# Attention feeding a bilinear layer on one core: the first conversions' Abs kept in order, three loads on another queue, PV and reciprocals moved ahead of the feed-forward slices

## The chip, the cores and the metric

One core of one Trainium2 chip. The metric is the device time of one execution in microseconds (us); lower is better. Before the change the median of three runs is 761.27 us (760.38 to 761.89).

## What is computed

Softcapped attention, then a bilinear feed-forward layer, all in fp32 (weights arrive as 64-bit floats):

```python
scores = cap * tanh((q @ k.T / sqrt(64)) / cap)      # 4 batches, 12 heads, 448 tokens, 64 wide
attn = exp(scores - max) / (sum + 1e-9)
x = (attn @ v) as 1792 tokens x 768
out = ((x @ w_a) * (x @ w_b)) @ w_out                # d_ff 1536
```

## The kernel before, in words

The 48 heads are worked as 24 **pairs** (two heads share the 128 partitions). Pairs 0 to 11 are group 0, pairs 12 to 23 group 1; a group gives 896 tokens of x. The kernel has three stretches: pairs 0 to 11 alone; pairs 12 to 23 beside the feed-forward of group 0; the feed-forward of group 1 alone.

The loop over `pi` (L478) runs a string of steps, one letter each: **P** `prep_pair(pi+1)` (transposes q and k on VectorE, L213; from pair 12 on splits them into a high and a low part), **S** and **T** `scores` for the first and second half of the keys (two PSUM tiles each: matmuls L239 or L244/L247, tanh on ScalarE L248, one exp L249, then sums of the probabilities on VectorE L253, or L256 and L257), **A** `attend(pi-1)` (PV matmuls L269, L271), **N** `normalize(pi-1)` (row sums by matmul L282, reciprocal L290, stored to DRAM L291 and read back spread over all partitions as `den` L295), **M** `scale` (L301, PV times `den`; pinned in program order on VectorE), **F** a slice of the feed-forward (`run_ffn`, matmuls L403 to L405 and L434 to L436). From pair 13 on the string is `SFANFMTPF`: three feed-forward slices a pair.

Score tiles and, in the second stretch, the PV tile (`both`, L261) come from one PSUM pool of two buffers (`ps_sc`): while PV is held, from A to M, the scores have one buffer.

Weights: `load64` (L327) fetches a 768 KB chunk of 64-bit weights into one of two buffers; `ready_w` (L347) turns it into fp32: ScalarE Copy L361 and Abs L362, three VectorE operations L363 to L365, a GpSimd add L366, a store to DRAM L367; `split_w` (L372) makes high and low parts (L385, L386). In program order the first two chunks are loaded at the end of pi = 2 and the first four converted at the ends of pi = 8 to 11, three of them split at the end of pi = 11.

The order on each engine is not the program's: a planner lays it out at build time from its own estimates of durations, taking at each moment the ready instruction that is earliest in the program. `keep_in_program_order` pins one instruction behind the instruction traced before it on its engine. Pinned before the change: L361, L301 and the first two weight loads (on SP's queue). The Abs L362 is not pinned, and needs only its chunk's load and a free buffer. On the chip each engine keeps the planned order: an instruction that waits holds all behind it.

Of the kernel before, what the change touches and what calls it, by code (L numbers as in the profile page):

```python
# [14 lines left out]
AF = mybir.ActivationFunctionType  # L15
# [102 lines left out]
def kernel(  # L118
# [11 lines left out]
    nc = tc.nc  # L130
# [3 lines left out]
    P = 128  # L134
# [11 lines left out]
    NPG = NPAIR // NG  # L146
# [5 lines left out]
    AHEAD = 4  # L152
# [10 lines left out]
    capt = top.tile([P, 8], F32, tag="capt", name="capt")  # L163
# [13 lines left out]
    def f32(ap):  # L177
        return ap.bitcast(F32)
# [14 lines left out]
    def load_pair(pi):  # L193
        b, hp = divmod(pi, NP)
        for nm, src in (("k", k), ("q", q)):
            t = ld.tile([P, S // BLK, BLK], F32, tag=f"ld{nm}", name=f"ld{nm}_{pi}")
            for j in range(2):
                for h in range(D // BLK):
                    rows = slice(j * D + h * BLK, j * D + (h + 1) * BLK)
                    cols = src[b, 2 * hp + j, :, h * BLK : (h + 1) * BLK]  # L200
                    eng = nc.scalar if nm == "q" and pi == 0 else nc.sync
                    eng.dma_start(t[rows], cols.rearrange("(c p) d -> p c d", p=BLK))
            raw[nm, pi] = t
        t = ld.tile([P, 2 * NC3 + 1, D], F32, tag="ldv", name=f"ldv_{pi}", bufs=3)
        nc.sync.dma_start(t, v[b, 2 * hp : 2 * hp + 2].rearrange("j s d -> (j s) d").rearrange("(c p) d -> p c d", p=P))
        raw["v", pi] = t

    def prep_pair(pi):
        stk[pi] = []
        for nm in "kq":  # L210
            t = raw.pop((nm, pi))
            tt = qk.tile([P, S], F32, tag=f"t{nm}", name=f"t{nm}_{pi}")
            nc.vector.transpose(tt, t.rearrange("p c d -> p (c d)"))  # L213
            if pi >= NPG:
                hi = qk.tile([P, S], F32R, tag=f"h{nm}", name=f"h{nm}_{pi}", bufs=1)
                lo = qk.tile([P, S], F32R, tag=f"t{nm}", name=f"l{nm}_{pi}")
                nc.scalar.copy(hi, tt)
                nc.vector.tensor_sub(lo, tt, f32(hi))
                tt = (hi, lo)
            stk[pi].append(tt)  # L220
        if pi >= NPG:
            for z, x in zip(kz, stk[pi][0]):
                for j, o in enumerate(own):
                    nc.gpsimd.tensor_copy(z[o, j * R : (j + 1) * R], x[o, krem[j] : krem[j] + R])
# [73 lines left out]
    def scale(pi):  # L298
        g, r = divmod(pi, NPG)
        t, den = pvs.pop(pi)  # L300
        tc.keep_in_program_order(nc.vector.tensor_mul(den, t[:, :S], den))  # L301
        if g == 0:
            split_x(r, den, nc.gpsimd)
        else:
            nc.sync.dma_start(xd[r], den)
# [21 lines left out]
    def load64(eng):  # L327
        t = pos["raw"]
        if t >= NW:
            return  # L330
        pos["raw"] += 1
        nm, f, _ = seq[t]
        cs = slice(f * P, (f + 1) * P)
        w = {"a": w_a, "b": w_b, "o": w_out}[nm].bitcast(I32)
        rt = wp.tile([P, DM, 2], I32, tag="w64", name=f"w64{nm}_{f}", bufs=2)
        if nm == "o":
            ld64 = eng.dma_start(rt.rearrange("p n t -> p (n t)"), w[cs, :])
        else:
            ld64 = eng.dma_start(
                rt.rearrange("p (k f) t -> p k (f t)", k=NK),  # L340
                w.rearrange("(k p) f -> p k f", p=P)[:, :, 2 * f * P : 2 * (f + 1) * P],
            )
        if t < 2:
            tc.keep_in_program_order(ld64)
        wraw[t] = rt

    def ready_w():  # L347
        t = pos["conv"]
        if t >= len(seq):
            return  # L350
        pos["conv"] += 1
        nm, f, g = seq[t]
        if g:
            wt = wp.tile([P, DM], F32, tag="wt", name=f"wr{nm}_{f}", bufs=AHEAD)
            nc.sync.dma_start(wt, wd[nm, f])
            wfull[t] = wt
            return
        rt = wraw.pop(t)
        hw, lw = rt[:, :, 1], rt[:, :, 0]
        wt = wp.tile([P, DM], I32, tag="wt", name=f"wt{nm}_{f}", bufs=AHEAD)  # L360
        tc.keep_in_program_order(nc.scalar.activation(lw, lw.bitcast(U32), AF.Copy, scale=2.0**-29))  # L361
        nc.scalar.activation(f32(wt), f32(hw), AF.Abs)  # L362
        nc.vector.tensor_scalar_max(f32(wt), f32(wt), TINY_HI)  # L363
        nc.vector.tensor_scalar(wt, wt, 3, 0x3FFFFFFF, op0=ALU.logical_shift_left, op1=ALU.bitwise_and)
        nc.vector.scalar_tensor_tensor(wt, hw, -0x40000000, wt, op0=ALU.bitwise_and, op1=ALU.bitwise_or)  # L365
        nc.gpsimd.tensor_tensor(wt, wt, lw, op=ALU.add)  # L366
        nc.gpsimd.dma_start(wd[nm, f], f32(wt))  # L367
        wfull[t] = f32(wt)
        while pos["raw"] < min(t + 3, NW):
            load64(nc.gpsimd)  # L370
# [75 lines left out]

    with ExitStack():
        load_pair(0)
        nc.sync.dma_start(capt[:, 3:4], cap.rearrange("(a b) -> a b", b=1).to_broadcast([P, 1]))
        make_identity(nc, ident)  # L450
        load_pair(1)
        nc.vector.memset(sel, 0.0)
        for z in kz:
            nc.vector.memset(f32(z), 0.0)
        for m in range(2):
            nc.vector.memset(sel[:, m, m * Q // 2 : (m + 1) * Q // 2], 1.0)
        nc.vector.tensor_scalar_mul(capt[:, 4:5], capt[:, 3:4], -1.0)
        nc.vector.tensor_max(capt[:, 5:6], capt[:, 3:4], capt[:, 4:5])
        nc.vector.tensor_scalar(bounded, capt[:, 5:6], CAP_MAX, None, op0=ALU.is_le)
        nc.vector.tensor_scalar_min(capt[:, 0:1], capt[:, 5:6], CAP_MAX)  # L460
        nc.vector.reciprocal(capt[:, 6:7], capt[:, 0:1])
        nc.vector.tensor_scalar_mul(capt[:, 1:2], capt[:, 6:7], 1.0 / math.sqrt(D))
        nc.scalar.activation(capt[:, 7:8], capt[:, 0:1], AF.Exp, scale=-1.0)
        nc.vector.tensor_scalar_mul(capt[:, 2:3], capt[:, 7:8], 1e-9 / R)

        gen, done, p0 = None, 0.0, 0
        total = NF * 72 * S + NTI * 2 * NF * 3 * HALF

        def run_ffn(upto):
            nonlocal gen, done  # L470
            while gen is not None and done < upto:
                try:
                    done += next(gen)
                except StopIteration:
                    gen = None

        prep_pair(0)
        for pi in range(NPAIR + 1):  # L478
            order = "PASMNFTF" if pi < NPG - 1 else "ASMNFTPF" if pi <= NPG else "SFANFMTPF"
            slices = 0  # L480
            for step in order:
                if step == "P" and pi + 1 < NPAIR:
                    prep_pair(pi + 1)
                elif step == "A" and pi > 0:
                    attend(pi - 1)
                elif step == "N" and pi > 0:
                    normalize(pi - 1)
                elif step == "M" and (pi > NPG or pi > 1):
                    scale(pi - (1 if pi > NPG else 2))
                elif step == "S" and pi < NPAIR:  # L490
                    scores(pi, 0)
                    if pi + 2 < NPG - 1:
                        load_pair(pi + 2)
                elif step == "T" and pi < NPAIR:
                    scores(pi, 1)
                elif step == "F":
                    slices += 1
                    run_ffn(total * (pi - p0 + slices / order.count("F")) / (NPG + STRETCH))
            if pi == 2:
                load64(nc.sync)  # L500
                load64(nc.sync)
            if NPG - AHEAD <= pi < NPG:
                ready_w()
            if pi == NPG - 1:
                for _ in range(3):
                    split_w()
            if NPG - 1 <= pi + 2 < NPAIR:
                load_pair(pi + 2)
            if pi == NPG:
                scale(pi - 1)  # L510
            if pi and pi % NPG == 0:
                run_ffn(1e18)
                gen, done, p0 = ffn(pi // NPG - 1), 0.0, pi + 1
        run_ffn(1e18)
# [37 lines left out]
```

## Time and profile before

| | us |
|---|---|
| median of three runs | 761.27 |
| the profiled execution | 764.42 |
| its span, first to last instruction | 762.6 |
| PE (TensorE matmul) busy in the span | 717.4 |
| DVE (VectorE) busy | 454.7 |
| ACT (ScalarE) busy | 338.1 |
| POOL (GpSimd) busy | 256.0 |

Times in rows are microseconds from the span's start unless marked ns. PE is the matmul side of TensorE, SPq and POOLq are the instructions that issue DMAs. In a timeline row stand start, duration, engine, line, operation, written tile <- read tiles, count, and in brackets the idle time of the engine just before, with what ended it. The first feed-forward matmul (L403) runs at 127.0, the scaling of the last pair at 463.8. A busy share is an average over stretches with different limits, so a wait is read in the stretch in which it lies.

### The profile page before, as it was taken

How to read it: one execution, taken by the hardware profiler on the slowest of the kernel's cores; microseconds unless marked ns; L12 is line 12 of the kernel's file. 1: busy time of each engine (PE TensorE's matmuls, PEld its weight loads, DVE VectorE, ACT ScalarE, POOL GpSimd, SP SyncE). 2: the span in 40 equal slices, each digit the busy share in tenths (PEclk: the TensorE clock that was granted, in tenths of full speed). 3: DMA queues.
4: the chain of work that ended last, by engine and by line, in shares of the span. 5: the costliest groups of instructions: out<-in, count | busy, mean ns of one | idle time of the engine just before them, and what ended most of it. 6: DMA issues, size and time to landing. Idle time of an engine off the chain costs nothing.

```text
span 762.6 us, 10299 instructions
## 1 busy us (share of the span) xinstructions
PE 717.4 (94%) x3948; PEld 568.8 (75%) x3948; DVE 454.7 (60%) x588; ACT 338.1 (44%) x426; POOL 256.0 (34%) x220
## 2 busy tenths in 40 slices
PE   6979878998999999999979999999999999999996
PEld 2322224677677787778768789899999999999996
DVE  4788899987855798686777755732113333243222
ACT  5777888565765665375445541022322102202200
POOL 0011467486624775075561441012101201200100
PEclk9999989999999999999999999999999999999999
DMA  7585678666664577252452333632112102201012
GB/s 129 110 171 117 143 171 207 161 172 211 170 176 127 162 206 218 57 159 98 149 199 87 104 114 121 219 97 80 43 41 83 63 14 69 83 21 42 1 42 107
DMA packets 136951, 90.49 MB, mean 119 GB/s; under 512 B 114624, under 2 KB 122560, under 8 KB 136896
## 3 DMA queue, kind: packets, MB, share of 16 engines
q1 hardware_dynamic: 125856, 48.64, 25.7%
q0 software_dynamic: 9184, 40.90, 16.1%
q8 instruction: 33, 0.54, 0.3%
q10 hardware_dynamic: 1856, 0.23, 0.2%
q14 instruction: 22, 0.18, 0.1%
HBM read 67.24 MB, written 22.50 MB: 118 GB/s over the span
## 4 chain that ended last, share of the span: by engine, by line
PE 62%; DMA 15%; DVE 10%; issue 4%; SPq 3%; ACT 3%; POOL 3%; DVEq 0%; POOLq 0%; ACTq 0%
PE pha L404 7%; PE pha L403 6%; PE pha L405 6%; PE phb L405 6%; PE phb L403 6%; PE phb L404 6%; PE po L436 5%; PE po L434 5%; PE po L435 5%; PE pv L269 3%; DMA w64a<-in_moe_w_a_dram 3%; DMA rd<-rec 2%; DMA xl<-xd 2%; DMA ldq<-in_q_dram 2%; PE psc L244 2%
## 5 line engine op out<-in xcount | busy, mean ns | idle before, releaser
L434 PE MATMUL po<-who,gh 128*128 128x384 f32 x336 | 114.6, 341 | 5.3 <-DVE acc L440 3.3
L436 PE MATMUL po<-who,gl 128*128 128x384 f32 x336 | 113.2, 337 | 0.1
L435 PE MATMUL po<-wlo,gh 128*128 128x384 f32 x336 | 112.9, 336 | 0.0
L404 PE MATMUL pha<-xlo,wha 128*128 128x448 f32 x288 | 105.2, 365 | 0.0
L403 PE MATMUL pha<-xhi,wha 128*128 128x448 f32 x288 | 105.0, 364 | 0.0
L405 PE MATMUL phb<-xhi,wlb 128*128 128x448 f32 x288 | 104.9, 364 | 0.0
L403 PE MATMUL phb<-xhi,whb 128*128 128x448 f32 x288 | 104.8, 364 | 0.0
L404 PE MATMUL phb<-xlo,whb 128*128 128x448 f32 x288 | 104.7, 364 | 0.0
L405 PE MATMUL pha<-xhi,wla 128*128 128x448 f32 x288 | 104.5, 363 | 0.0
L248 ACT ACTIVATE pf<-psc,capt 128x896 f32<-128x896 f32 x96 | 84.8, 909 | 23.5 <-PE psc L239 9.3
L249 ACT ACTIVATE pf<-pf,capt 128x1792 f32<-128x1792 f32 (+1 forms) x48 | 77.0, 1605 | 0.9
L386 POOL TENSOR_TENSOR wlb<-wrb,whb 128x768 fp32r<-128x768 f32 x12 | 22.2, 1847 | 156.5 <-PE pha L405 142.1
L434 PEld LDWEIGHTS po<-who,gh 128*128 128x128 f32 x336 | 63.3, 188 | 10.2 <-DVE acc L440 4.8
L440 DVE TENSOR_TENSOR acc<-po,acc 128x384 f32<-128x384 f32 x84 | 45.4, 551 | 39.0 <-PE po L436 39.0
L410 DVE TENSOR_TENSOR asb<-phb,asb 128x448 f32<-128x448 f32 x48 | 29.6, 617 | 64.6 <-PE phb L405 64.6
L269 PE MATMUL pv<-pf,ldv 128*64 128x448 f32 x288 | 65.2, 567 | 1.3 <-ACT pf L249 1.0
L436 PEld LDWEIGHTS po<-who,gl 128*128 128x128 f32 x336 | 63.3, 188 | 1.8 <-issue 1.0
L435 PEld LDWEIGHTS po<-wlo,gh 128*128 128x128 f32 x336 | 63.4, 189 | 0.8 <-issue 0.6
L412 DVE TENSOR_TENSOR gl<-asb,gh 128x448 fp32r<-128x448 f32 x48 | 51.0, 1063 | 20.5 <-ACT gh L411 20.5
L411 ACT CAST gh<-asb 128x448 fp32r<-128x448 f32 x48 | 27.1, 565 | 80.7 <-DVE asb L410 80.5
L239 PE MATMUL psc<-tq,tk 64*128 64x448 f32 (+1 forms) x192 | 49.7, 623 | 12.6 <-DVE tq L213 7.0
L403 PEld LDWEIGHTS pha<-xhi,wha 128*128 128x128 f32 x288 | 53.9, 187 | 6.3 <-issue 1.7
(99 smaller groups left out, 1191.9 us busy)
## 6 DMA issues: line engine op xcount, KB each, us to landing
w64o<-in_moe_w_out_dram POOLq DMA_DIRECT2D x12, 768.0 KB, 5.9
w64a<-in_moe_w_a_dram POOLq DMA_DIRECT2D x11, 768.0 KB, 5.7
w64b<-in_moe_w_b_dram POOLq DMA_DIRECT2D x11, 768.0 KB, 6.6
ldk<-in_k_dram SPq DMA_DIRECT2D x96, 56.0 KB
ldv<-in_v_dram SPq DMA_DIRECT2D x24, 224.0 KB
den<-rd SPq DMA_DIRECT2D x48, 112.0 KB
ldq<-in_q_dram SPq DMA_DIRECT2D x92, 56.0 KB
out_dram<-acc SPq DMA_DIRECT2D x13, 384.0 KB
```

The source lines that it names most:

```text
L239: nc.tensor.matmul(to, tk[o, at : at + (P if n == 2 else R)], tq[o], start=True, stop=True)
L248: nc.scalar.activation(pf[:, 2 * i : 2 * i + n], psc[:, :n, :S], AF.Tanh, scale=capt[:, 1:2])
L249: nc.scalar.activation(pf, pf, AF.Exp, scale=capt[:, 0:1])
L269: nc.tensor.matmul(t[j * D : (j + 1) * D, :S], tv[:, j * (NC3 + 1) + c], p, start=(c == 0), stop=False)
L403: nc.tensor.matmul(t[:, :S], wh[:, kk], xhi[:, kk, cs], start=(kk == 0), stop=False)
L404: nc.tensor.matmul(t[:, :S], wh[:, kk], xlo[:, kk, cs], start=False, stop=False)
L405: nc.tensor.matmul(t[:, :S], wl[:, kk], xhi[:, kk, cs], start=False, stop=(kk == NK - 1))
L412: nc.vector.tensor_sub(gl[:, cs], asb[h], f32(gh[:, cs]))
L434: nc.tensor.matmul(t[:, :HALF], gh[:, cs], wh, start=(f == fs[0]), stop=False)
L435: nc.tensor.matmul(t[:, :HALF], gh[:, cs], wl, start=False, stop=False)
L436: nc.tensor.matmul(t[:, :HALF], gl[:, cs], wh, start=False, stop=(f == fs[-1]))
L440: nc.vector.tensor_add(acc[:, ti, hs], t[:, :HALF], acc[:, ti, hs])
```

## The change

Three places. The Abs of the first four conversions is pinned in program order. The load of `cap` at the start and the first two weight loads go from SP's queue to GpSimd's. From pair 13 on the steps are `SANFFMTPF` instead of `SFANFMTPF`: PV and normalization come directly behind the first half of the scores, and two feed-forward slices stand between the normalization and the scaling, with as many slices a pair as before.

```diff
@@ ready_w, L361
         tc.keep_in_program_order(nc.scalar.activation(lw, lw.bitcast(U32), AF.Copy, scale=2.0**-29))
-        nc.scalar.activation(f32(wt), f32(hw), AF.Abs)
+        mag = nc.scalar.activation(f32(wt), f32(hw), AF.Abs)
+        if t < AHEAD:
+            tc.keep_in_program_order(mag)
@@ start, L448
         load_pair(0)
-        nc.sync.dma_start(capt[:, 3:4], cap.rearrange("(a b) -> a b", b=1).to_broadcast([P, 1]))
+        nc.gpsimd.dma_start(capt[:, 3:4], cap.rearrange("(a b) -> a b", b=1).to_broadcast([P, 1]))
         make_identity(nc, ident)
@@ loop over pi, L479
-            order = "PASMNFTF" if pi < NPG - 1 else "ASMNFTPF" if pi <= NPG else "SFANFMTPF"
+            order = "PASMNFTF" if pi < NPG - 1 else "ASMNFTPF" if pi <= NPG else "SANFFMTPF"
@@ loop over pi, L499
             if pi == 2:
-                load64(nc.sync)
-                load64(nc.sync)
+                load64(nc.gpsimd)
+                load64(nc.gpsimd)
```

`AHEAD` is 4, `NPG` is 12.

## Rows read from the trace of the kernel before

**Rows 1.** The page: busy us and shares; busy tenths in 40 slices.
```profile
PE 717.4 (94%) x3948; PEld 568.8 (75%) x3948; DVE 454.7 (60%) x588; ACT 338.1 (44%) x426; POOL 256.0 (34%) x220
PE   6979878998999999999979999999999999999996
```
**Rows 2.** Windows: length, busy PE, PEld, DVE, ACT, POOL; PEclk, DMA share, GB/s.
```profile
38.00:53.00 15.00, 10.36 (x56) 3.24 (x54) 11.27 (x17) 10.79 (x11) 1.39 (x1) 0.89 0.89 192
53.00:85.00 32.00, 30.30 (x194) 9.67 (x194) 27.95 (x37) 26.39 (x25) 5.66 (x4) 1.00 0.57 112
85.00:127.00 42.00, 31.61 (x186) 10.08 (x184) 40.03 (x44) 33.62 (x37) 29.17 (x23) 0.88 0.73 190
205.00:464.00 259.00, 251.46 (x1440) 200.58 (x1437) 177.39 (x223) 139.46 (x181) 124.60 (x115) 1.00 0.47 142
```
**Rows 3.** Waits of PE, 7 to 127: total us, times, longest.
```profile
PE sum L282 <- DVE psum L257: 9.2, 9, 2.4
```
**Rows 4.** Waits of PE, 127 to 460.
```profile
PE psc L247 <- ACT pf L248: 5.2, 3, 3.0
PE psc L247 <- DVE den L301: 1.0, 1, 1.0
PE psc L244 <- DVE den L301: 1.0, 2, 0.6
```
**Rows 5.** Timeline, 36 to 44.
```profile
36.32 0.59 SPq L339 DMA_DIRECT2D w64a<-in_moe_w_a_dram  x1
...
41.39 0.89 ACT L362 ACTIVATE wta<-w64a 128x768 f32<-128x768 f32 x1 [6.26 <-DMA w64a<-in_moe_w_a_dram]
...
43.23 3.36 PE L239 MATMUL psc<-tq,tk 64*128 64x448 f32 x8 [4.32 <-ACT pf L248]
```
**Rows 6.** Timeline: the first scores of pairs 3, 8 and 9.
```profile
30.34 1.77 PE L239 MATMUL psc<-tq,tk 64*128 64x448 f32 x8
...
77.24 1.77 PE L239 MATMUL psc<-tq,tk 64*128 64x448 f32 x8
...
84.77 1.77 PE L239 MATMUL psc<-tq,tk 64*128 64x448 f32 x8
```
**Rows 7.** Conversions: on DVE by line (ns min/median/max), and timeline.
```profile
L363 DVE TENSOR_SCALAR wta<-wta x12: 534/560/2084, 42.3 to 394.1; 128x768 f32<-128x768 f32 x12
...
L365 DVE SCALAR_TENSOR_TENSOR wta<-w64a,wta x12: 947/959/2501, 48.1 to 396.0; 128x768 int32<-128x768 int32 x12
...
85.23 0.90 ACT L361 ACTIVATE w64a<-w64a 128x768 int32<-128x768 uint32 x1
...
99.23 2.21 POOL L366 TENSOR_TENSOR wtb<-wtb,w64b 128x768 int32<-128x768 int32 x1
...
99.78 2.08 DVE L363 TENSOR_SCALAR wta<-wta 128x768 f32<-128x768 f32 x1
```
**Rows 8.** By line: first scores and their tanh, pair 14, then pair 23.
```profile
L244 PE MATMUL psc<-hq,lk x4: 362/364/364, 163.3 to 163.8; 64*128 64x448 f32 x4
...
L248 ACT ACTIVATE pf<-psc,capt x1: 1019/1019/1019, 166.7 to 166.7; 128x896 f32<-128x896 f32 x1
...
L244 PE MATMUL psc<-hq,lk x4: 362/363/364, 423.0 to 423.4; 64*128 64x448 f32 x4
...
L248 ACT ACTIVATE pf<-psc,capt x2: 999/1002/1005, 424.4 to 425.3; 128x896 f32<-128x896 f32 x2
```
**Rows 9.** Timeline: reciprocal of pair 13, scaling of pair 19.
```profile
179.10 0.84 DVE L290 RECIPROCAL rec<-pv 128x112 f32<-128x112 f32 x1
...
354.09 0.62 DVE L301 TENSOR_TENSOR den<-pv,den 128x448 f32<-128x448 f32 x1 [6.99 <-DMA den<-rd]
```
**Rows 10.** The moved transfers: timeline at the start; weight loads on POOL, ns.
```profile
4.12 0.56 SPq L449 DMA_DIRECT2D capt<-in_cap_dram  x1
...
8.94 1.01 ACT L248 ACTIVATE pf<-psc,capt 128x896 f32<-128x896 f32 x1 [0.77 <-PE psc L239]
...
L339 POOL DMA_DIRECT2D w64a<-in_moe_w_a_dram x11: 846/846/880, 91.4 to 383.9; - x11
```

## The prediction

> **What bounds the kernel now.** I read the busy shares first, then the same by stretch, then who TensorE waits for in each stretch, and last the timeline around the longest waits. PE is busy 717.4 of 762.6 us and full in nearly every slice from the eighth on; the thin slices lie before it [rows 1]. So the end is set by PE's own work plus its holes, and a change pays only by closing holes or by removing half-speed time. The holes are in two places. Up to 127 us (pairs 0 to 11 alone) PE waits 9.2 us in nine pieces for VectorE's probability sums [rows 3] and once 4.3 us for a tanh [rows 5]. From 127 to 460 us, where attention runs beside the feed-forward, PE waits 5.2 us for tanhs and 2.0 us for the scaling [rows 4]; in the long window 205 to 464 it is idle only 259 - 251.5 = 7.5 us [rows 2]. Behind 464 nothing is changed.
>
> **The Abs, and the stall it makes.** The planner floated the first Abs (L362) far ahead: ScalarE sits 6.26 us idle until the first weight chunk lands at 41.39 and holds the tanhs behind it; TensorE's next scores, which need the PSUM tile that a tanh frees, start 4.32 us late [rows 5]. Behind that hole the eight score matmuls take 3.36 us, against 1.77 for the same eight undisturbed [rows 5, 6]. The granted clock over 38 to 53 is 0.89: 2 x 0.11 x 15 = 3.3 us at 1.2 GHz instead of 2.4, which costs half, 1.65 us [rows 2]. Directly, pinning is worth 4.32 + 1.65 = 6.0 us. The whole disturbance is larger: six pairs go from 30.34 to 84.77, 54.4 us, and at the undisturbed 84.77 - 77.24 = 7.53 us a pair they would take 45.2 [rows 6]. That bounds the gain at 9.2 us. I take the middle of 6.0 and 9.2, about 7.6, because the load itself still runs in that window and keeps some of the disturbance.
>
> **Where the pinned work goes.** L361 is already pinned and starts its first conversion at 85.23 [rows 7]. Two Abs and the six VectorE operations behind them, done at 41 to 51 us before, now come there. ScalarE gets 2 x 0.9 us more on 33.6 of 42 us: hidden in its 8.4 idle us. VectorE is the problem: it is busy 40.03 of the 42 us from 85 to 127 [rows 2], and PE's waits there are for it [rows 3]. Undisturbed, L363 and L364 take 0.56 us each and L365 0.96, so two chunks are 2 x 2.08 = 4.2 us [rows 7]. Lower end 0 (it fits into the idle 2 us and what can be done beside the first feed-forward matmuls, where PE is full), upper end 4.2 plus blocking (the first rival). I take 4.2, since 95% busy is nearer to full than to free. First stretch: -7.6 + 4.2 = **-3.4 us**. The third and fourth Abs move by a few us inside the saturated stretch: 0, since VectorE covers it; should VectorE not be the limit, a wait of the third for its load could go too.
>
> **The queues.** The load of `cap` costs SP 0.56 us of issue at 4.12 [rows 10]. The first tanh waits for scores at 8.94, not for `cap` [rows 10], so moving it is worth 0; it would cost if GpSimd's copy landed after 8.9, for which no row speaks. The pair loads behind it on SP start 0.6 us sooner, which at most trims the first pairs by that. The first two weight loads leave SP (0.59 us for the first) for GpSimd at 0.85 each [rows 5, 10]; GpSimd is 1.4 of 15 us busy there [rows 2], so this is hidden, and pair loads on SP no longer stand behind 1.5 MB of weights. Pinned only behind GpSimd's first subtraction they may start sooner than before, beside a read-back of `den`, and delay it. The upper end of that: VectorE held at L301 as long as in the worst such wait, 6.99 us [rows 9], less the room it has (32 - 27.95 = 4.05 us from 53 to 85, [rows 2]), 3 us. I take 0 for all of it, from -0.6 to +3.
>
> **The new order from pair 13 on.** Nothing is added or taken away: PV (16 matmuls), sums, one reciprocal, one store and two read-backs on SP, and the scaling are the same. N moves one slice ahead of M and T; the pairs' first scores come (423.0 - 163.3) / 9 = 28.9 us apart [rows 8], of which three slices are the larger part, so a slice is an estimated 7 us. **For it:** the reciprocal of pair 13 runs at 179.10, the scaling of pair 19 keeps VectorE waiting 6.99 us for its read-back [rows 9]; with a second slice between N and M that wait is covered, the PV tile is given back before T, and T finds two PSUM tiles instead of one. At stake are the 5.2 + 2.0 = 7.2 us of [rows 4]. **Against it:** PV now takes the PSUM tile that the first tanh of S frees, with no slice between. In pair 14 the score matmuls end at 163.8 + 0.36 = 164.2 and that tanh at 166.7 + 1.02 = 167.7, 3.6 us later; in pair 23 it is 423.4 + 0.36 = 423.8 to 425.4, 1.6 us. Over the ten pairs 14 to 23 these gaps sum to 17 us [rows 8]. What the planner foresees of a gap it fills with feed-forward matmuls; only what it does not foresee is a hole. The nearest row is the same kind of wait in T: 5.2 us of holes in the whole stretch [rows 4]. So the new exposure is about 5.2 us, the old one of 7.2 mostly goes: -7.2 + 5.2 = -2.0, of which I take **-1.5**. Ends: -9 (all 7.2 gone and the half-speed time beside them) and +17 (nothing filled).
>
> **Sum.** -3.4 - 1.5 + 0 = -4.9. The profiled execution took 764.42 us, its span 762.6, so 1.8 lie around it; it stands 3.15 above the median. 764.42 - 4.9 = 759.5 for it, and on the median 761.27 - 4.9 = **756.4 us**. A run can be told from no change at about 0.2%, 1.5 us.
>
> **Rival one: the conversions are blocked, and all is given back.** At 99.78 one L363 took 2.08 us instead of 0.56, just behind a GpSimd add L366 that began at 99.23 and ran 2.21 [rows 7]. In the new place the four single-input operations of the first two chunks lie beside such adds. If all four are held, that is 4 x 1.5 = 6.1 us more: -7.6 + 4.2 + 6.1 - 1.5 = +1.2, **762.5 us**. The Trainium skill has the rule for this: its page "SBUF — State Buffer", section "SBUF: two separate sides", says that VectorE in a two-port mode and GpSimd share one pair of ports under a lock, and that whichever comes second is blocked for the other's whole instruction. By that rule the trace agrees at 99.78; but the median of L363 over its twelve is 0.56 [rows 7], so most escape. Chance 0.15.
>
> **Rival two, the slower side: PV waits behind its own scores.** If the planner believes ScalarE free and it is not (a weight conversion waiting for its load stands ahead of the tanh, as in [rows 5]), PV goes out directly and PE stands still. With half of the 17 us unforeseen and nothing of the 7.2 won: -3.4 + 8.5 = +5.1, **766.4 us**. It decides from 4.9 us of holes on (then the sum is over +1.5). Against it: the planner left only 5.2 us of such holes before. Chance 0.20.
>
> **Rival three: all waits of the second stretch close.** -3.4 - 9 = -12.4, **748.9 us**. Chance 0.13. And the planner may lay PV where it lay before whatever the letters say: then only the first stretch pays, -3.4, 757.9, which I count to my forecast.
>
> **How the numbers follow.** My forecast, about 752 to 759.7, has 0.52. Faster by over 0.2% (below 759.7): 0.52 + 0.13 = 0.65. Within 0.2%: rival one, 0.15. Slower: 0.20. The range goes from 748.5 (rival three) to 765 765 (into rival two's case), leaving out some 0.15 in all.
>
> **What would show it.** Right: no Abs before 75 us, no PE hole near 39 us, and a granted clock of 1.00 from 38 to 53; the first scores of pair 9 at about 77; VectorE still over 90% busy from there to the first feed-forward matmul, at about 124 instead of 127; reciprocals within 2 us of their sums in the second stretch, and the waits for L301 gone. The forecast is wrong if PE shows waits "PV <- tanh" of over 5 us in total from 127 to 460, if L363 and L364 run at 2 us in the first chunks, or if the first feed-forward matmul is not earlier than 127.

## The result and the profile after

The changed kernel takes 771.41 us (median of four runs, 769.22 to 772.43) against 761.58 (760.38 to 762.68): a ratio of **1.0113, 95% interval 1.0085 to 1.0141**, so it is slower, and 6 us above the top of the range. The profiled execution took 771.69 us, its span 769.9 (764.42 and 762.6 before). From L363 on, lines stand two higher than before: L363 to L368 are now L365 to L370, L434 and L440 are L436 and L442.

The page, busy shares and slices, which answer to [rows 1], with the granted clock of PE as third line:

```profile
PE 721.7 (94%) x3948; PEld 574.2 (75%) x3948; DVE 450.0 (58%) x588; ACT 338.4 (44%) x426; POOL 253.6 (33%) x223
...
PE   5969977999989998999989999999999999999996
...
PEclk9979987999999998999999999999999999999999
```

The same windows as [rows 2], same columns:

```profile
38.00:53.00 15.00, 8.45 (x48) 2.61 (x46) 8.12 (x11) 6.35 (x6) 1.49 (x1) 0.75 0.82 159
53.00:85.00 32.00, 32.00 (x198) 10.06 (x196) 27.01 (x37) 26.86 (x26) 5.65 (x4) 0.96 0.56 113
85.00:127.00 42.00, 32.26 (x179) 10.23 (x175) 37.64 (x47) 33.31 (x36) 27.28 (x23) 0.92 0.78 174
205.00:464.00 259.00, 247.82 (x1395) 198.87 (x1392) 179.75 (x221) 138.91 (x179) 124.39 (x117) 0.97 0.47 141
```

The window that was to be mended, 38 to 53, is worse: PE busy 8.45 us instead of 10.36, its clock 0.75 instead of 0.89. The long window is worse too: idle 259 - 247.82 = 11.2 us instead of 7.5, clock 0.97 instead of 1.00. The waits of PE, 7 to 127 and then 127 to 460 (total us, times, longest), against [rows 3, 4]:

```profile
PE sum L282 <- DVE psum L257: 10.0, 5, 6.5
...
PE po L436 <- DVE acc L442: 5.6, 2, 3.7
PE sum L282 <- DVE psum L257: 4.2, 1, 4.2
PE po L436 <- ACT acc L440: 2.8, 1, 2.8
PE po L436 <- ACT gh L413: 2.5, 2, 1.5
...
PE psc L247 <- DVE den L301: 1.1, 1, 1.1
```

The waits of the score tiles on the tanh, 5.2 us in [rows 4], are gone, as hoped; in their place PE waits at `po`, the feed-forward's output tiles. In the first stretch one wait of 6.5 us stands some 7 us behind the place where the tanh's 4.32 was. The timeline around it, 33 to 51 (answers to [rows 5]), and pair 9's first scores (to [rows 6]):

```profile
33.99 0.86 POOL L339 DMA_DIRECT2D w64a<-in_moe_w_a_dram  x1
...
34.73 1.20 SPq L295 DMA_DIRECT2D den<-rd  x2
34.85 0.84 POOL L339 DMA_DIRECT2D w64b<-in_moe_w_b_dram  x1
...
37.22 5.84 SPq L202 DMA_DIRECT2D ldq<-in_q_dram  x4
...
43.93 0.62 DVE L301 TENSOR_TENSOR den<-pv,den 128x448 f32<-128x448 f32 x1 [7.27 <-DMA den<-rd]
...
49.85 0.98 PE L282 MATMUL sum<-psum,sel 128*32 128x112 f32 x16 [6.55 <-DVE psum L257]
...
85.76 1.77 PE L239 MATMUL psc<-tq,tk 64*128 64x448 f32 x8
```

No Abs is there any more. But the two weight loads, 1.5 MB, go out on either side of the read-back of `den`; its data release VectorE's pinned L301 only at 43.93, after 7.27 us, and everything behind it on VectorE, up to the sums that PE needs, is late. The four q loads took SP 5.84 us to issue (1.99 where nothing disturbs them). So pair 9 starts at 85.76, not at 77, and the first feed-forward matmul runs at 130.3 (127.0 before). Of the 7.3 us that the span grew, 3.3 lie before that matmul and 4.3 between it and the first feed-forward matmul of group 1 (a stretch of 369.1 us before, of 373.4 after); what comes behind is 0.3 shorter. The forecast had -3.4 and -1.5 for the two.

### The profile page after: what moved, and what is told of

Same layout as the page of the kernel before. It is cut to its first block, busy times and chain, and to the rows that moved or that the text cites. A ratio compares the mean times of both kernels' runs of the same rounds, so it can differ in the third digit from the quotient of the medians.

```text
span 769.9 us, 10300 instructions
## 1 busy us (share of the span) xinstructions
PE 721.7 (94%) x3948; PEld 574.2 (75%) x3948; DVE 450.0 (58%) x588; ACT 338.4 (44%) x426; POOL 253.6 (33%) x223
## 4 chain that ended last, share of the span: by engine, by line
PE 51%; DMA 4%; DVE 2%; POOL 2%; issue 1%; ACT 1%; POOLq 0%; ACTq 0%
PE po L436 6%; PE po L438 5%; PE po L437 5%; PE pha L406 5%; PE pha L407 5%; PE pha L405 5%; PE phb L405 5%; PE phb L407 5%; PE phb L406 5%; DMA xl<-xd 2%; DMA w64a<-in_moe_w_a_dram 2%; PE pv L269 2%; PE psc L244 1%; DVE xlo L311 1%; PE pv L271 1%
## 5 line engine op out<-in xcount | busy, mean ns | idle before, releaser
L436 PE MATMUL po<-who,gh 128*128 128x384 f32 x336 | 116.1, 346 | 12.1 <-DVE acc L442 6.8
L438 PE MATMUL po<-who,gl 128*128 128x384 f32 x336 | 115.2, 343 | 0.2
L437 PE MATMUL po<-wlo,gh 128*128 128x384 f32 x336 | 115.0, 342 | 0.0
L436 PEld LDWEIGHTS po<-who,gh 128*128 128x128 f32 x336 | 64.7, 192 | 16.8 <-DVE acc L442 8.7
L442 DVE TENSOR_TENSOR acc<-po,acc 128x384 f32<-128x384 f32 x84 | 45.6, 552 | 40.7 <-PE po L438 40.6
L414 DVE TENSOR_TENSOR gl<-asb,gh 128x448 fp32r<-128x448 f32 x48 | 53.3, 1111 | 21.0 <-ACT gh L413 20.9
L239 PE MATMUL psc<-tq,tk 64*128 64x448 f32 (+1 forms) x192 | 49.6, 617 | 11.4 <-DVE tq L213 7.4
```

What stands on the lines that cost most here:

```text
L239: nc.tensor.matmul(to, tk[o, at : at + (P if n == 2 else R)], tq[o], start=True, stop=True)
L414: nc.vector.tensor_sub(gl[:, cs], asb[h], f32(gh[:, cs]))
L436: nc.tensor.matmul(t[:, :HALF], gh[:, cs], wh, start=(f == fs[0]), stop=False)
L437: nc.tensor.matmul(t[:, :HALF], gh[:, cs], wl, start=False, stop=False)
L438: nc.tensor.matmul(t[:, :HALF], gl[:, cs], wh, start=False, stop=(f == fs[-1]))
L442: nc.vector.tensor_add(acc[:, ti, hs], t[:, :HALF], acc[:, ti, hs])
```

## The experiments

Each run stands beside runs of the kernel before on the same chip, so ratios are compared, not times. From each run's profile I take two more numbers: the first feed-forward matmul, and what the **second stretch** loses, from there to the last scaling: PE's idle time plus half of its busy time at a granted clock of 1.2 GHz, summed over the matmul rows (half, since in [rows 5, 6] eight score matmuls take 3.36 us behind the hole and 1.77 undisturbed). Each is one execution. By the last scaling the kernels with the new order have done less of the feed-forward (1186 matmul rows in the change, 1203 before), so what a stretch loses is compared, and where its length matters it is taken up to group 1's first feed-forward matmul.

| run | ratio (95%) | first FFN matmul | idle + half of slow busy = lost |
|---|---|---|---|
| before | 1 | 127.0 | 12.3 + 3.4/2 = 14.0 |
| the change | 1.0113 (1.0085 to 1.0141) | 130.3 | 13.5 + 15.7/2 = 21.4 |
| e1 Abs alone | 1.0045 (1.0011 to 1.0079) | 132.2 | 9.8 + 10.8/2 = 15.2 |
| e2 order alone | 1.0076 (1.0043 to 1.0108) | 126.9 | 14.9 + 15.2/2 = 22.5 |
| e3 loads alone | 1.0079 (1.0049 to 1.0109) | 128.3 | 13.3 + 9.3/2 = 17.9 |
| e4 change, loads on SP | 1.0148 (1.0075 to 1.0221) | 130.9 | 12.7 + 22.7/2 = 24.1 |
| e5 Abs, thirds | 1.0003 (0.9978 to 1.0028) | 128.4 | 12.2 + 3.2/2 = 13.8 |
| e6 order, third buffer | 1.0087 (1.0055 to 1.0118) | 135.0 | 11.7 + 9.9/2 = 16.6 |
| e7 third buffer | 1.0141 (1.0095 to 1.0188) | 134.8 | 12.4 + 15.7/2 = 20.2 |
| e8 PV early only | 1.0046 (1.0015 to 1.0077) | 128.6 | 13.9 + 11.3/2 = 19.5 |
| e9 thirds, Abs free | 1.0105 (1.0061 to 1.0149) | 136.1 | 13.3 + 6.8/2 = 16.7 |
| e10 scaling a slice later | 1.0017 (0.9988 to 1.0046) | 127.8 | 11.4 + 10.2/2 = 16.5 |
| e11 Abs, thirds on GpSimd | 0.9991 (0.9968 to 1.0014) | 128.7 | 10.5 + 10.9/2 = 16.0 |
| e12 Abs, thirds, conversions early | **0.9969 (0.9948 to 0.9991)** | 127.3 | 11.9 + 3.4/2 = 13.6 |
| e13 order, no late loads | 1.0031 (1.0004 to 1.0058) | 134.0 | 8.7 + 9.0/2 = 13.2 |
| e14 no late loads | 1.0013 (0.9983 to 1.0042) | 135.1 | 6.3 + 9.0/2 = 10.8 |
| e15 e12 with the order | 1.0033 (1.0000 to 1.0066) | 127.0 | 15.2 + 9.4/2 = 19.9 |
| e16 e12, thirds on GpSimd | 0.9981 (0.9955 to 1.0007) | 126.4 | 13.3 + 9.9/2 = 18.2 |
| e17 e15, adds pinned | 1.0015 (0.9994 to 1.0037) | 127.5 | 14.9 + 10.6/2 = 20.2 |
| e18 e12, adds pinned | 1.0048 (1.0025 to 1.0071) | 127.9 | 11.2 + 11.0/2 = 16.7 |

### The parts of the change, one by one

**e1**, the pin on the Abs alone:

```diff
-        nc.scalar.activation(f32(wt), f32(hw), AF.Abs)
+        mag = nc.scalar.activation(f32(wt), f32(hw), AF.Abs)
+        if t < AHEAD:
+            tc.keep_in_program_order(mag)
```

> Only the Abs of the first four conversions is pinned; loads, cap and order as before the change. Theory of the loads (the two weight loads, issued from GpSimd ahead of the read-back of den, hold VectorE and make the new 6.55 us hole at 43 us): here the loads stand behind den on SP as before, so no Abs before 75 us, no PE hole over 2 us between 36 and 50, first feed-forward matmul at 122 to 124 instead of 127.0, total 756 to 759 us. Rival, pinning itself is the loss (the conversions come into a full VectorE): first feed-forward matmul at 127 or later, total 761 or more.

Slower by 0.45%. The old hole at 39 is gone, pair 5 starts at 48.0 instead of 52.8; then comes a hole of 6.06 us one pair later. The timeline, 36 to 60:

```profile
39.57 3.23 SPq L202 DMA_DIRECT2D ldq<-in_q_dram  x2
...
45.59 0.58 SPq L291 DMA_DIRECT2D rd<-rec  x1
...
52.63 0.62 DVE L301 TENSOR_TENSOR den<-pv,den 128x448 f32<-128x448 f32 x1 [6.79 <-DMA den<-rd]
...
58.55 0.97 PE L282 MATMUL sum<-psum,sel 128*32 128x112 f32 x16 [6.06 <-DVE psum L257]
```

SP issues in order, and slowly while the 1.5 MB are on the way (3.23 us for two q loads): the store of the reciprocals waits behind them until 45.59, so `den` comes back at 52.6. Pair 9 starts at 87.1 (84.8 before), and from there to the first feed-forward matmul 45.1 us pass instead of 42.2: the moved conversions cost about 2.9.

**e2**, the order alone (`SANFFMTPF` in place of `SFANFMTPF`):

> Only the order of the steps from pair 13 on is changed. Theory that the new order costs the second stretch (holes at feed-forward output matmuls while ScalarE or VectorE waits for a weight load, and half-speed time behind each): first stretch as before (first feed-forward matmul at 127.0), but 127 to 464 longer by 4 to 7 us, holes of 2 us and more at the output matmuls, three or four half-speed windows instead of one; total 765 to 769 us. Rival, the second stretch is only disturbed by what happens in the first: total within 2 us of 761.5.

Slower by 0.76%; the first stretch is as before, the second loses 22.5 us instead of 14.0. Idle time grew by only 2.6 of that; the rest is PE's busy time at 1.2 GHz.

**e3**, the two weight loads on GpSimd alone (`load64(nc.gpsimd)` twice), and **e4**, the whole change but with these two on SP:

> Only the two first weight loads go to GpSimd's queue; the Abs stays unpinned, cap on SP, order as before. Theory of the loads: they start at about 34 us, ahead of den; VectorE waits at L301 for 5 to 8 us around 37 to 44 (3.0 at most before), and as the Abs waits for the same loads, the two holes lie on each other: first feed-forward matmul 1 to 4 us later than 127.0, total 762 to 766. Rival, the queue is immaterial: VectorE's wait at L301 under 3 us, total within 1.5 us of 761.5.

> The changed kernel with its two first weight loads back on SP's queue (Abs pinned, cap on GpSimd, new order). Theory of the loads: the 7.27 us wait of VectorE at L301 falls to 2 us or less and PE's 6.55 us hole goes, first feed-forward matmul at 122 to 125 instead of 130.3; total 6 to 9 us under the changed kernel's 771.4, so 762 to 765, of which what stays above e1 is the new order's. Rival, the hole is due to the pinned Abs or the order: it stays, total 769 to 772.

Both are slower. In e3, L301 waits 6.79 us at 43.42 and PE has two holes of 3.6 us; in e4 L301 waits 7.54 us at 52.66 and PE 6.8. So the stall is there on either queue, with the loads ahead of a read-back of `den` on GpSimd's and one pair later on SP's: what makes it are the bytes. The Trainium skill has the rule that fits this on its page "DMA: Bandwidth & Descriptors", section "Issuing engines are not separate DMA queues": transfers started by different engines run on the same 16 DMA engines, and another issuer saves only issue time. The traces of e3 and e4 agree: 6.79 and 7.54 us. The earlier start on GpSimd's queue is not free, though: with the Abs as before, e3 costs 0.79%, of which its one profile, among its fastest runs, shows 1.3 us before the first feed-forward matmul and 2.1 between that and group 1's.

The third piece, the load of `cap` on GpSimd's queue, was not run alone. In the two profiles that have it the first scores come at 7.41 and 7.32 us, in the others at 6.71 to 7.13; by pair 3 (30.66 and 30.57, against 30.04 to 30.81) nothing of that is left to see.

### The burst

**e5**: Abs pinned, order of before, and the first two chunks loaded in thirds, one part a pair:

```diff
+        if t < 2:
+            for i in range(3):
+                parts.append((
+                    rt.rearrange("p (k f) t -> p k (f t)", k=NK)[:, 2 * i : 2 * i + 2],
+                    w.rearrange("(k p) f -> p k f", p=P)[:, 2 * i : 2 * i + 2, 2 * f * P : 2 * (f + 1) * P],
+                ))
...
+            if parts and pi >= 2:
+                tc.keep_in_program_order(nc.sync.dma_start(*parts.pop(0)))
```

> Abs pinned as in the change, the order of before, and each of the first two 768 KB weight chunks loaded in three parts of 256 KB, one part behind each pair from pair 2 on, on SP. Theory burst (the 1.5 MB sent at once make the den read-backs late, whichever queue issues them): no hole of over 2 us between 36 and 60 us, no wait of VectorE for L301 over 4 us there, pair 9's first scores at about 78 (84.8 before), the first feed-forward matmul at about 123 (127.0 before; the pinned conversions still cost 4 to 5 us from 85 on), total about 757 to 759. Rival, the Abs stall was only a part of a wider disturbance and the bytes delay the chain however they are spread: a hole of 4 to 7 us split over several pairs, first feed-forward at 128 to 132, total 764 to 768.

The hole is gone: L301's waits there are 1.3 to 3.1 us. But pair 9 starts at 82.8, not 78, and the first feed-forward matmul runs at 128.4: the bytes cost less, not nothing (8.75 us a pair from pair 3 to 9 where 7.53 is undisturbed), and 45.6 us from pair 9 on show the conversions again, 3.4 over the 42.2 of before. Even with the kernel before; the theory's 757 to 759 was missed.

**e9**: the thirds with the Abs left free, **e11**: e5 with the thirds on GpSimd (`nc.gpsimd.dma_start(*parts.pop(0))`), **e12**: e5 with the conversions earlier:

```diff
-            if NPG - AHEAD <= pi < NPG:
+            if pi in (NPG - 6, NPG - 4, NPG - 2, NPG - 1):
                 ready_w()
```

> The kernel before with the first two chunks loaded in thirds, one a pair on SP, and nothing pinned: the planner now lays the two floating Abs into pairs 5 and 8, behind the last third of each. Theory, the pinned conversions cost and the pinned Abs brings nothing by itself: no hole of over 3 us between 36 and 60, pair 9's first scores at about 82 as with thirds and the pin (82.8), but the first feed-forward matmul about 3 us earlier than there, at 125 (128.4 with the pin), total 757 to 761. Rival, the pin is free and the first stretch is set by the bytes: first feed-forward at 128 again, total 763 to 765. Rival, a floating Abs waits for its last third as it did for the whole chunk: a ScalarE wait of over 3 us at L368 and a PE hole of 3 to 4 us behind it, total 762 to 766.

> Abs pinned, thirds as before, but issued on GpSimd instead of SP (order of before). Theory queue (in pairs 2 to 7 SP's queue is about 6.2 of 7.5 us full, and every issue more delays the den read-back): pair 9's first scores at 79 to 80 (82.8 with the thirds on SP), first feed-forward at 125, total 759 to 762. Theory bytes (256 KB more a pair delay the transfers whichever queue sends them): pair 9 at 82 to 84, first feed-forward at 128 to 129, total 763 to 766.

> Abs pinned and thirds on SP, and the four conversions of the first stretch put into pairs 6, 8, 10 and 11 instead of 8, 9, 10 and 11 (order of before). Theory, VectorE's full stretch from 85 us is where the pinned conversions cost: the first chunk's 2.1 us go into a pair where VectorE has room, first feed-forward at 126 to 127 (128.4 with 8 to 11), total 760 to 763. Rival, the third load, which is now sent two pairs earlier, beside the last thirds, gives it back: first feed-forward at 128 to 131, total 763 to 767.

e9 is the strongest of these. Waits of ScalarE from 30 to 127, where L368 is the Abs in e9's numbering, and the PE wait behind them:

```profile
ACT wta L368 <- DMA w64a<-in_moe_w_a_dram: 7.6, 1, 7.6
ACT wtb L368 <- DMA w64b<-in_moe_w_b_dram: 4.5, 1, 4.5
...
PE pv L269 <- ACT pf L249: 10.4, 5, 5.4
```

A free Abs stands before its last third too. Against e5 it costs 1.0105 - 1.0003 = 1.0%, 7.8 us (against e11, on the same chip, 1.1%): **so much is the pin worth once the burst is spread**, and the theory that the pin brings nothing by itself fell. e11 against e5 is within their intervals: with thirds, too, SP's issue time is not the price. e12 beats both kernels, by 0.31% against the one before: the first chunk is converted at 65.9, before VectorE is full, and the first feed-forward matmul comes at 127.3 instead of 128.4. It is the best of eighteen variants, its interval only just leaves out 1, and its one profile, with a span of 762.1 against 762.6, hardly shows where the gain lies. **e16**, e12 with the thirds on GpSimd, is no better:

> Abs pinned, thirds issued on GpSimd, conversions in pairs 6, 8, 10 and 11, order of before. If what the thirds still cost is SP's issue time: first feed-forward at 125 to 126 (127.3 with SP), total 761 to 763. If it is the bytes: 127 to 128, total 763.5 to 765.

### The order

**e8** and **e10** try its two sides, as far as a string allows. e8, `SAFNFMTPF`, puts PV alone ahead of the first slice; the row sums, the reciprocal and the normalization (all in N) stay behind it. e10, `SFANFFMTP` up to pair 23, leaves A and N where they were and puts a second slice between N and the scaling, taken from the end of the pair. Neither moves N ahead of the first slice, as the change does:

> Of the new order only the half that moves the probability sums' matmuls, PV and the reciprocal ahead of the next slice (A directly behind S); the normalization stays behind that slice, as before. Theory one, A directly behind S is what costs: 768 to 771, as with the whole new order, with holes of 3 to 4 us in the second stretch. Theory two, the early normalization costs (VectorE stands at L301 for the read-back of den with the feed-forward's accumulations behind it): 761 to 764, no such holes. Theory three, neither by itself, both are the late weight load: anything from 763 to 768, with each hole of over 2 us beside a conversion that waits for its load.

> The other half of the new order alone: the probability sums and PV stay behind the first slice, and the normalization is put straight behind them, with two slices between it and the scaling. Theory one, the early reciprocal and a later scaling cost nothing and A behind S is what costs: second stretch loses 13 to 16 (14.0 before), no hole of over 3 us near 300, total 760 to 764. Theory two, both halves cost by moving VectorE's and ScalarE's queues against the weight loads: lost 18 to 20, total 765 to 768, with a hole at a feed-forward output matmul behind a conversion that waits for its load.

The first costs 0.46%, the second 0.17%, which is less than its interval; the whole order costs 0.76. They are no exact halves, so the sum of 0.63 proves nothing. Where the time goes, the changed kernel's timeline from 283 to 304 shows:

```profile
284.86 2.51 DVE L365 TENSOR_SCALAR wtb<-wtb 128x768 f32<-128x768 f32 x1
...
289.96 1.84 POOL L368 TENSOR_TENSOR wtb<-wtb,w64b 128x768 int32<-128x768 int32 x1 [3.02 <-issue]
...
292.68 0.84 POOL L339 DMA_DIRECT2D w64a<-in_moe_w_a_dram  x1
...
299.98 0.89 ACT L361 ACTIVATE w64a<-w64a 128x768 int32<-128x768 uint32 x1 [4.50 <-DMA w64a<-in_moe_w_a_dram]
...
301.73 0.87 DVE L365 TENSOR_SCALAR wta<-wta 128x768 f32<-128x768 f32 x1 [2.38 <-issue]
...
302.52 0.54 DVE L442 TENSOR_TENSOR acc<-po,acc 128x384 f32<-128x384 f32 x1
...
303.12 0.69 PE L436 MATMUL po<-who,gh 128*128 128x384 f32 x1 [3.70 <-DVE acc L442]
```

Read from below: PE's hole of 3.70 us waits for an accumulation that VectorE has behind a weight operation; that waits for ScalarE's conversion, which waits 4.50 us for a load; the load went out only at 292.68, since the add L368 that gives its buffer free was late. From within the hole on, from 301.4 to 308.2, the granted clock was 1.2 GHz. The same chunk in e2, where the first stretch is as before, and in the kernel before (L366 is the add):

```profile
287.79 1.85 POOL L366 TENSOR_TENSOR wtb<-wtb,w64b 128x768 int32<-128x768 int32 x1 [3.02 <-issue]
...
290.51 0.85 POOL L339 DMA_DIRECT2D w64a<-in_moe_w_a_dram  x1
...
298.32 0.88 ACT L361 ACTIVATE w64a<-w64a 128x768 int32<-128x768 uint32 x1 [5.06 <-POOL wto L366]
```

```profile
282.33 2.24 POOL L366 TENSOR_TENSOR wtb<-wtb,w64b 128x768 int32<-128x768 int32 x1
...
285.44 0.85 POOL L339 DMA_DIRECT2D w64a<-in_moe_w_a_dram  x1
...
290.85 0.94 ACT L361 ACTIVATE w64a<-w64a 128x768 int32<-128x768 uint32 x1
```

The load goes out 5.1 us later, while the feed-forward is where it was: its first output matmul of this group runs at 286.05 in e2 and 286.55 before. Up to 256 us e2's loads go out at most 1 us later than those of before, mostly earlier; from 269 on all are later, by 3.3 to 6.5 us up to 370 and by 1.7 to 5.9 behind. Between, in all four profiles with the new order and that stretch's loads as before (the change, e2, e4, e15), GpSimd does a `wto` add ahead of a `wtb` add, at 263 and 267 in e2; in before, e1, e3, e5, e8 to e12 and e16 the `wtb` add comes first. (With the loads changed, in e7 and e14 below, the old order has the `wto` add first too.)

**e6** gives the raw chunks a third buffer and issues each load one chunk earlier, with the new order; **e7** is the same with the old one. The space comes from the second half's probability tile (and from the identity matrix, which this path does not use and which is now made only in the other one):

```diff
-        pf = pp.tile([P, 4 - hf, S], F32, tag=f"pf{hf}", name=f"pf_{pi}_{hf}")
+        pf = pp.tile([P, 4 - hf, S], F32, tag=f"pf{hf}", name=f"pf_{pi}_{hf}", bufs=PFB - hf)
...
-        rt = wp.tile([P, DM, 2], I32, tag="w64", name=f"w64{nm}_{f}", bufs=2)
+        rt = wp.tile([P, DM, 2], I32, tag="w64", name=f"w64{nm}_{f}", bufs=3)
...
-        while pos["raw"] < min(t + 3, NW):
+        while pos["raw"] < min(t + 4, NW):
```

> The new order alone, with a third buffer for raw weight chunks so that each load is issued one chunk earlier; paid for by the second half's probability tile having one buffer less. Theory late loads (ScalarE stands at a weight conversion for its load, and the new order only moves where TensorE meets that): the holes of 3 to 4 us at the feed-forward's output matmuls near 213, 299 and 400 go, and with them the half-speed stretches behind them; time lost from the first feed-forward matmul to the last scaling about 12 (22.5 with the new order alone, 14.0 before), total 758 to 762. Rival, the order itself costs (PV and the reciprocals in place of a slice make TensorE wait for VectorE's accumulations): lost stays at 20 to 24, total 768 to 772.

> The order of before with the third raw buffer and the earlier loads (and the second half's probability tile with one buffer less): the control for the run beside it. Theory late loads: total 757 to 761, lost in the second stretch 10 to 13 against 14.0 before, and no more than 2 us from the run with the new order. Rival, the loads are early enough before: 763 plus whatever the buffer taken away costs, lost 14 or more.

In total both miss: a third load now goes out at 34 us just ahead of the other two, and the first feed-forward matmul comes 8 us later. In the second stretch ScalarE waits 6.7 us for raw loads where in e2 it was 51, the hole near 300 is gone, and the new order loses 16.6 us instead of 22.5; what is left are holes of 3.1 us at 196 and 4.5 at 362, the second for `den`. The kernel before waits 48 us for raw loads too, so the two orders do not differ in the sum of these waits, at most in where they fall. And the old order loses 20.2 here, and the tile that was made smaller may be why. So e6 and e7 speak for the loads without settling it. **e13** and **e14** leave every raw load after the first four out, with the new order and the old; a chunk is converted from the tile of two chunks before, so the weights behind the fourth chunk and the output are other than the reference's:

```diff
+        if t >= AHEAD:
+            wraw[t] = kept[t % 2]
+            return
...
+        kept[t % 2] = rt
```

> The new order alone, with every raw weight load after the first four left out: the conversions run over the four chunks that are there, so all the feed-forward's weights after them, and the output, are other than the reference's; every instruction of the engines stays. Theory late loads (the new order brings VectorE's weight operations later, so the raw buffer comes free later, the next load goes out later, and ScalarE stands at the next conversion with tanhs and casts behind it): without the loads the second stretch loses 8 to 13 us, no PE hole of over 3 us near 300, total 755 to 760, and within 2 us of the run beside it with the old order. Rival, the order itself (PV and the sums before the slice make TensorE wait for VectorE, whatever the loads do): lost stays at 18 or more, and 5 us or more above the run beside it.

> The order of before with the same loads left out: the control. Theory late loads: the second stretch loses 8 to 13 us (14.0 before), total 755 to 760, within 2 us of the run with the new order, on either side. Rival, the order itself: as here 755 to 760, but 5 us or more below the run with the new order.

Without the loads the two orders come close: from the first feed-forward matmul to group 1's the new one needs 363.1 us and the old one 361.1, where with the loads it was 376.5 (e2) and 369.1 (before); they lose 13.2 and 10.8, and the totals lie 1.5 us (0.18%) apart, in overlapping intervals. (The totals themselves missed: two more conversions slid into the first stretch, which became 7 to 8 us longer.) So **without the loads most of the order's price is gone**; whether a rest of 1 to 2 us is its own, these runs cannot tell. **e15**, the order on top of e12:

> Abs pinned, thirds, conversions in pairs 6, 8, 10 and 11 as in the run that beat the kernel before, with the new order: the change as it was, with its first stretch mended. If the order's cost is its own, it comes on top: 763.9 + 6 = 770, ratio 1.004 to 1.008, lost in the second stretch 19 to 24. If it comes from the disturbed first stretch that hands over late, it goes: 764 to 766, lost 14 to 17.

1.0033 against 0.9969, 0.64% or 4.9 us (0.52% against e16, which ran on the same chip), and the same hole again (3.72 us from 296.5 on): the price does not come from the disturbed first stretch. **e17** and **e18** pin the adds on e15 and on e12:

```diff
-        nc.gpsimd.tensor_tensor(wt, wt, lw, op=ALU.add)
+        tc.keep_in_program_order(nc.gpsimd.tensor_tensor(wt, wt, lw, op=ALU.add))
```

> The run with the mended first stretch and the new order, with one thing more: the GpSimd add that ends each conversion is pinned in program order. In the four profiles with the new order the planner lays one third-matrix add in front of the second-matrix add near 263 us, where every profile with the old order has them the other way round, and the next raw load goes out 5 us later. Theory swap: with the pin the second-matrix add is in front again, the load behind it goes out by 265, the hole of 3 to 4 us near 300 is gone, the second stretch loses 14 to 17 (19.9 without the pin), ratio 0.996 to 1.000. Rival, the swap is only a sign of a chain that is late anyway: GpSimd waits at the pinned add, the hole near 300 stays or moves, lost 19 to 24, ratio 1.003 or more.

> The same pin with the mended first stretch and the order of before: the control. Theory swap: the old order has no such swap near 263, so the pin does little, ratio 0.995 to 0.999 (0.9969 without the pin), lost 13 to 16, and within 0.3 per cent of the run with the new order and the pin. Rival: 0.5 per cent or more below the run with the new order and the pin.

Both expectations of the theory failed in part. With the pin the `wtb` add is first (263.30) and its load goes out at 266.03 instead of 269.23, but the later adds wait, the next load is later (274.19 instead of 271.19), and the hole stays, 3.02 us from 296.3 on. The old order loses by the pin (0.9969 to 1.0048). So the swapped add is a sign of the late chain and not its cause. With the adds pinned the new order is no longer the slower one, 1.0015 against 1.0048 in slightly overlapping intervals, although its one profiled execution loses more (20.2 and 16.7). So much can a single profile differ: the eight kernels with the old order, the chain unpinned and the second stretch's loads as before lose 13.6 to 18.2 us, the four with the new one 19.9 to 24.1.

**What stays open:** which instruction of the conversion chain decides. Shown is that the order's price is 0.64 to 0.76% with the chain as the planner lays it, that it is 0.18% and not clear of nothing with the loads away, and that it is gone with the adds pinned. That late loads make the price is argued from the traces and not shown: every one of these edits also makes the planner lay all queues anew, and no run holds that layout fixed.

## Why the prediction was wrong

**The Abs and its stall (-7.6): the step that failed first.** The stall was rightly read, and its direct price of 6.0 us was near: pinned alone (e1), pair 5 starts 4.8 us earlier. (The 7.8 us of e9 against e5 come from another stall, two waits for last thirds of 7.6 and 4.5 us; that they lie near 7.6 is chance.) What failed is the sentence that "the load itself still runs in that window and keeps some of the disturbance", priced at a share of the difference between 6.0 and 9.2. In truth there were two stalls on top of each other: ScalarE's wait for the chunk, and the lateness of `den` through the same 1.5 MB. The Abs hid the second, because nothing could be late for PE while PE stood anyway. So e1, 4.8 us ahead at pair 5, is 2.3 us behind at pair 9. The bound of 9.2 us from [rows 6] took the whole disturbance for the Abs' own; no row of before could divide it, so its lower end should have been near 0 or below.

**The moved conversions (+4.2).** Right in kind, a little high: from pair 9 to the first feed-forward matmul the kernel takes 42.2 us before, 45.1 in e1, 45.6 in e5, so 2.9 to 3.4. e12, with an earlier pair, has its first feed-forward matmul 1.1 us before e5's.

**The queues (0, from -0.6 to +3).** The mechanism stood in the text: the loads ahead of a read-back of `den`, VectorE held at L301 "as long as in the worst such wait, 6.99 us". It was held 7.27. Wrong was to take 0, and to set the room of the window 53 to 85 against it: there is no room at 44, where PE's next sums hang on VectorE directly. That the loads are "hidden" because GpSimd is idle counted the issuing engine, not the bytes. It is the burst that was mis-priced, not the move from queue to queue: with the Abs pinned, the loads on SP cost no less (e4, where VectorE was held 7.54 us); with the Abs free, the move does cost (e3).

**The new order (-1.5, from -9 to +17).** Its direction was wrong: +0.64 to 0.76%, 5 to 6 us. The first half of the argument held in part: of the score tiles' waits, 5.2 us on the tanh and 2.0 on L301 before, 1.1 us on L301 are left; with the order alone (e2), though, those on L301 are 4.0. The price did not come where rival two put it, at PV behind its own scores (no wait of PV for a tanh is among PE's from 127 to 460). The cause it names, a weight conversion that stands waiting for its load, does stand before the hole near 300, but what is held there are the feed-forward's accumulations; whether it makes the whole price stays open. And the sum counted idle time, while most of what the stretch lost more is half-speed time: idle time 12.3 before and 13.5 after, busy time at 1.2 GHz 3.4 and 15.7. The same idle time in a few holes of 3 us cost more than in many short ones.

**Rival one (blocked conversions)** did not happen: the four operations that it priced (L365 and L366 of the first two chunks) take 0.55 to 0.56 us; of the first four L365 one takes 1.63. The total lies beyond rival two (766.4), since both stretches went wrong and no case had that.

## What to carry to other kernels

When a stall is taken away, ask what else was late at that moment for the same reason: two waits on one burst of traffic overlap, and the profile shows only the one that ends last. A large early load belongs in parts, spread over the steps that can carry it (with the pin and an earlier conversion 0.31% faster than before, the best version here, if only just clear of noise), and moving it to an idle engine's queue changes nothing of its bytes. A reordering that adds no work can still be dear, and a ring of two buffers, where each late reader makes the next load late, is the first place to look: check when each buffer comes free and when its next load goes out, not only who waits now.

## What the runs showed of the hardware that was not expected

The time to issue a transfer is not fixed. SP's four q loads took 1.99 us undisturbed and 5.84 beside the 1.5 MB, and since the queue is in order, in e1 a store of 3.5 KB whose reciprocals were ready at 40.3 went out only at 45.59. And the clock: at the changed kernel's hole of 3.70 us the granted clock was 1.2 GHz from 301.4 to 308.2, and it fell at three more holes there, within them or less than 1 us behind (holes of 4.2 us that ended at 129.4, 2.8 at 216.0, 1.9 at 399.5); in the kernel before it fell once there, from 189.9 to 193.3 at the end of the one hole of 3.0 us, and stayed at 2.4 GHz at five others of 1.05 to 1.64. Of the 7.4 us more that the stretch lost, 6.2 are this.
